# List-scheduled expert work, and seven block products instead of eight for the second expert matrix in two of three passes

## Chip, cores and metric

The kernel runs on one core of one Trainium2 chip. The metric is device time of one execution in microseconds (us). TensorE (PE) multiplies, VectorE (DVE), ScalarE (ACT) and GpSimd (POOL) do elementwise work, SyncE (SP) issues the DMAs.

## What is computed

```python
scores = scale * np.matmul(q, k.transpose(0, 1, 3, 2))       # 4 x 8 heads, 576 tokens, 64 wide
attn = np.matmul(scores * Dmat, v)                           # decaying causal retention
x = attn as (2304 tokens, 512)
h = x @ w_in                                                 # 512 -> 1024
solu = h * softmax(h); ln = layernorm(solu) * g_ln
x = ln @ w_out                                               # 1024 -> 512
for e in range(4):                                           # experts, all on every token
    h = np.maximum(x @ w1[e], 0.0)                           # first product, 512 -> 1024
    out += p[:, e:e + 1] * (h @ w2[e])                       # second product, 1024 -> 512
```

All is float32. Every operand of a large product is split in a high and a low part, and `mm3` adds three products for one (high by high, high by low, low by high).

## The kernel before

The 2304 tokens are 18 groups of 128 (`NG`), worked off in three passes of six groups. Passes are numbered 1 to 3 here (`p` is 0 to 2 in the code). A pass has a stage `h_mm` (x by `w_in`, softmax and norm, transposes by `t_mm`), a stage `x2_mm` (by `w_out`), and `experts`, which takes most of the time. The retention of groups 0 to 10 stands ahead of pass 1, interleaved by hand in the string `ORDER`; groups 11 to 17 are done at the start of the pass that needs them (`own_groups`).

**First product of an expert.** The token dimension, the input dimension and the hidden dimension are each cut in two, and the eight block products are replaced by seven with sums of blocks (Strassen-Winograd, `PRODUCTS`). On the weight side the sums are S1 to S4, on the token side T1 to T4. It goes in four quarters (`m` of `NM`), each of seven products of 2 x 3 matmuls of 384 columns: 168 matmuls. `l1` evicts them: ACT copies, DVE additions, then `relu_hi` on ACT and `relu_lo` on DVE make the split of h.

**Second product.** `l2_mm` multiplies a block of 128 tokens by all of `w2`: eight slices of the hidden dimension, three matmuls each, 512 columns. Six blocks make 144 matmuls. `l2_out` multiplies by the probability and adds to `acc`.

**Weights.** In every pass, and so three times, `w1_load` and `w1_ops` fetch `w1` (512 KB for each quarter), POOL forms S1 to S4, and ACT and DVE split the seven blocks into one of three slots of `wA`. `w2_ops` fetches 256 KB slices and splits them on ACT and POOL into `wB`. These operations are queued by hand between the products: `W1_SLOTS` and `W2_SLOTS` say after which product how many are issued. Every engine then works in the order of the code.

## Time and profile before

| | us |
|---|---|
| timed runs, median of 3 | 1056.38 |
| timed runs, lowest and highest | 1053.75, 1474.92 |
| profiled execution, first to last instruction (span) | 1052.0 |
| of it PE busy | 1029.9 (98%) |
| DVE, ACT, POOL busy | 537.4, 459.3, 346.7 |

The profile is of one execution. Its span leaves out what lies ahead of the first and behind the last instruction. Matmuls are pipelined, so their busy time overlaps: the cost of one is read from the distance of two starts, not from its duration.

### The profile page before, as it was taken

How to read it: one execution, taken by the hardware profiler on the slowest of the kernel's cores; microseconds unless marked ns; L12 is line 12 of the kernel's file. 1: busy time of each engine (PE TensorE's matmuls, PEld its weight loads, DVE VectorE, ACT ScalarE, POOL GpSimd, SP SyncE). 2: the span in 40 equal slices, each digit the busy share in tenths (PEclk: the TensorE clock that was granted, in tenths of full speed). 3: DMA queues.
4: the chain of work that ended last, by engine and by line, in shares of the span. 5: the costliest groups of instructions: out<-in, count | busy, mean ns of one | idle time of the engine just before them, and what ended most of it. 6: DMA issues, size and time to landing. Idle time of an engine off the chain costs nothing.

```text
span 1052.0 us, 15117 instructions
## 1 busy us (share of the span) xinstructions
PE 1029.9 (98%) x5996; PEld 929.6 (88%) x5996; DVE 537.4 (51%) x855; ACT 459.3 (44%) x872; POOL 346.7 (33%) x385
## 2 busy tenths in 40 slices
PE   5899999999999999999999999999999999999998
PEld 4788998998989888999898989988899989898996
DVE  6999764453635315565363544514556536354441
ACT  4478563342625206654262533403565426153430
POOL 2433443432433101443352334112143335233410
PEclk9999999999999999999999999999999999999999
DMA  9856531321212661112121212535412122121311
GB/s 348 340 208 221 198 123 60 90 64 67 81 40 81 254 266 72 41 54 67 61 80 41 80 60 90 200 141 208 203 41 61 60 71 70 40 89 56 88 39 50
DMA packets 35062, 118.56 MB, mean 113 GB/s; under 512 B 4144, under 2 KB 4144, under 8 KB 28848
## 3 DMA queue, kind: packets, MB, share of 16 engines
q1 hardware_dynamic: 34992, 117.60, 32.1%
q8 instruction: 47, 0.77, 0.3%
q14 instruction: 23, 0.19, 0.1%
HBM read 101.86 MB, written 15.73 MB: 112 GB/s over the span
## 4 chain that ended last, share of the span: by engine, by line
PE 92%; DVE 5%; DMA 2%; ACT 1%; issue 1%; SPq 0%; DVEq 0%; ACTq 0%
PE o L139 12%; PE o L140 12%; PE o L138 12%; PE l1x L138 6%; PE l1x L140 6%; PE l1x L139 6%; PE l1y L140 3%; PE l1y L139 3%; PE l1y L138 3%; PE x2ps L138 3%; PE x2ps L139 3%; PE x2ps L140 3%; PE hps L138 3%; PE hps L139 2%; PE hps L140 2%; PE l1z L140 2%
## 5 line engine op out<-in xcount | busy, mean ns | idle before, releaser
L140 PE MATMUL o<-wB,h 128*128 128x512 f32 x576 | 224.8, 390 | 0.0
L139 PE MATMUL o<-wB,h 128*128 128x512 f32 x576 | 224.7, 390 | 0.0
L138 PE MATMUL o<-wB,h 128*128 128x512 f32 x576 | 224.5, 390 | 0.0
L581 POOL TENSOR_TENSOR tmp<-tmp 128x256 f32<-128x256 f32 x192 | 156.2, 828 | 176.8 <-DVE wA L143 157.8
L143 POOL TENSOR_TENSOR wB<-tmp,wB 128x512 fp32r<-128x512 f32 x96 | 123.7, 1295 | 238.1 <-ACT wB L146 238.1
L146 ACT ACTIVATE wA<-tmp 128x512 fp32r<-128x512 f32 (+1 forms) x145 | 100.1, 704 | 173.3 <-DMA tmp<-in_w 110.6
L682 DVE SCALAR_TENSOR_TENSOR acc<-o,pr,acc 128x512 f32<-128x512 f32 x54 | 40.5, 751 | 204.5 <-PE o L140 204.5
L140 PEld LDWEIGHTS o<-wB,h 128*128 128x128 f32 x576 | 108.2, 188 | 22.4
L138 PEld LDWEIGHTS o<-wB,h 128*128 128x128 f32 x576 | 108.2, 188 | 22.0
L139 PEld LDWEIGHTS o<-wB,h 128*128 128x128 f32 x576 | 108.1, 188 | 21.7
L143 DVE TENSOR_TENSOR wA<-tmp,wA 128x512 fp32r<-128x512 f32 (+1 forms) x145 | 109.6, 778 | 4.5 <-ACT wA L146 4.5
L146 ACT ACTIVATE tmp<-l1x 128x384 f32<-128x384 f32 x96 | 47.1, 491 | 121.6 <-PE l1x L140 118.9
L138 PE MATMUL l1x<-xb,wA 128*128 128x384 f32 x288 | 96.7, 336 | 1.2 <-ACT tmp L146 1.2
L139 PE MATMUL l1x<-xb,wA 128*128 128x384 f32 x288 | 96.4, 335 | 0.0
L140 PE MATMUL l1x<-xb,wA 128*128 128x384 f32 x288 | 96.3, 335 | 0.0
L138 PE MATMUL x2ps<-h,wB 128*128 128x384 f32 x192 | 65.1, 339 | 0.4 <-DVE wA L377 0.4
L146 ACT ACTIVATE wB<-tmp 128x512 fp32r<-128x512 f32 x96 | 60.6, 631 | 9.9 <-DMA tmp<-in_w 9.9
L140 PE MATMUL x2ps<-h,wB 128*128 128x384 f32 x192 | 64.3, 335 | 0.0
L139 PE MATMUL x2ps<-h,wB 128*128 128x384 f32 x192 | 64.3, 335 | 0.0
L138 PE MATMUL l1y<-xa,wA 128*128 128x384 f32 x192 | 64.2, 335 | 0.0
L139 PE MATMUL l1y<-xa,wA 128*128 128x384 f32 x192 | 64.2, 335 | 0.0
L140 PE MATMUL l1y<-xa,wA 128*128 128x384 f32 x192 | 64.2, 334 | 0.0
(142 smaller groups left out, 1882.5 us busy)
## 6 DMA issues: line engine op xcount, KB each, us to landing
tmp<-in_w SPq DMA_DIRECT2D x48, 512.0 KB, 3.6
tmp<-in_w SPq DMA_DIRECT2D x96, 256.0 KB, 2.6
grps<-in_qkv SPq DMA_DIRECT2D x17, 1024.0 KB, 5.8
wA<-sin SPq DMA_DIRECT2D x8, 1024.0 KB, 6.9
wB<-sout SPq DMA_DIRECT2D x8, 1024.0 KB, 8.2
out<-acc SPq DMA_DIRECT2D x18, 256.0 KB, 2.1
grps<-in_qdec SPq DMA_DIRECT2D x16, 256.0 KB, 5.8
sin<-wA SPq DMA_DIRECT2D x4, 1024.0 KB, 7.7
```

Source lines behind the costliest of these rows:

```text
L138: nc.tensor.matmul(ps, lh, rh, start=first, stop=False, skip_group_check=more)
L139: nc.tensor.matmul(ps, lh, rl, start=False, stop=False, skip_group_check=more)
L140: nc.tensor.matmul(ps, ll, rh, start=False, stop=last, skip_group_check=more)
L143: (eng or nc.vector).tensor_tensor(out=dst, in0=src, in1=hi.bitcast(F32), op=ALU.subtract)
L146: nc.scalar.activation(out=dst, in_=src, func=AF.Copy)
L581: return lambda: nc.gpsimd.tensor_tensor(out=dst, in0=a, in1=b, op=op)
L682: nc.vector.scalar_tensor_tensor(out=a, in0=ps, scalar=sc, in1=a, op0=ALU.mult, op1=ALU.add)
```

## The change

**Order.** `nc` becomes a `Recorder`. From the second half of pass 1's `x2_mm` stage on, every operation is recorded with what it reads and writes; `flush` gives each a due time, counted back from when PE would need it, and issues them engine by engine, earliest due first, by a table of costs (`FIXED`, `RATE`). PE's own operations stay in the order of the code. The hand-made slots are gone.

**Pass 1** still computes the second product by eight block products. It forms and splits each `w1` quarter once, and stores the split blocks in DRAM (`w1_store`, 1792 KB for each quarter in runs of 1 KB). For `w2`, DVE adds S1 to S4 (`w2_next`, stored unsplit in runs of 512 bytes), and `w2_blocks` copies the three plain blocks from DRAM to DRAM.

**Passes 2 and 3** run `experts_s`. The first product is the same, from stored splits: one DMA of 256 KB for each of 28 products, 14 slots. The second product works on transposed tokens with seven block products for each of two output halves: 2 x 7 x 4 slices x 3 = 168 matmuls of 384 columns. Its weight blocks come unsplit from DRAM (14 of 256 KB, 6 slots) and are split again by ACT and POOL. Its token side needs T1 to T4 of h: eviction of the first product (`evict1`) grows by the subtractions into `Tf` and by splits of all seven blocks. `gather` multiplies by a row of probabilities and adds.

**Retention.** Groups 12 to 17 move from pass 3's start into pass 2's `h_mm` stage, and are stored in DRAM for pass 3.

```diff
+class Recorder:
...
+    def start(self):
+        self.ops = []
...
+    def flush(self, done=True):
+        ops, self.ops = self.ops, None if done else []
...
+        for op in ops:
+            op.after, op.due, op.at = [], None, clock
+            if op.engine == "PE":
+                op.due = clock
+                clock += op.cost
...
+        for op in reversed(ops):
+            due = min((s.due for s in op.after), default=None)
+            if due is None and op.engine != "PE":
+                due = op.at + SLACK
+            if due is not None:
+                due -= op.cost + LATENCY
+                op.due = due if op.due is None else min(op.due, due)
...
+        while len(order) < len(ops):
+            late = now + 1e-9
+            while waiting and waiting[0][0] <= late:
+                op = heapq.heappop(waiting)[2]
+                queue[op.engine].append((op.due, op.index, op))
...
+            for e in FIXED:
+                if free[e] > late or not queue[e] or (e == "SP" and self.dma > late + DEPTH):
+                    continue
+                can = [r for r in queue[e] if not (r[2].port and self.port > late)]
+                can = [r for r in can if all(busy.get(b, 0) <= late for b in r[2].banks)]
+                if e == "PE":
...
+                best = min(can)
+                queue[e].remove(best)
+                op = best[2]
+                moved = True
...
+                order.append(op)
...
+        for op in order:
+            op.call()
...
+SLACK = 12.0
+DEPTH = 2.0
...
+    ctx.enter_context(stack)
...
+    def open_pool(name, bufs):
+        stack.close()
+        new = stack.enter_context(tc.tile_pool(name=name, bufs=1, space=bass.MemoryType.PSUM))
+        width = 2048 // bufs
+        pool["a"] = [new.tile([P, width], F32, tag=f"a{i}", name=f"{name}_{i}") for i in range(bufs)]
+        pool["n"] = 0
...
+    def w1_store(s):
+        o = 3584 * (s % 3)
+        dst = s_w1[s].rearrange("p (b h t) -> h p b t", b=7, h=2)
+        for h in range(2):
+            src = wA[:, o + 1792 * h : o + 1792 * h + 1792].bitcast(F32)
+            nc.sync.dma_start(out=dst[h], in_=src.rearrange("p (b t) -> p b t", b=7))
+
+    def w2_blocks(e):
+        for m in range(2):
+            dst = s_w2[e][:, 3584 * m : 3584 * m + 1536].rearrange("p (a t) -> p a t", a=3)
+            nc.sync.dma_start(out=dst, in_=w2b[e, m].rearrange("a p t -> p a t"))
...
+    def w2_next(e, k):
+        raw = (w2s, area["wC"][:, 0:1024].rearrange("p (i t) -> p i t", i=2))[k % 2]
+        buf = area["wC"][:, 1024:2048]
+        s1, s2, s3, s4 = (buf[:, 256 * i : 256 * i + 256] for i in range(4))
+        a11, a21, a12, a22 = (raw[:, j, 256 * i : 256 * i + 256] for j in range(2) for i in range(2))
...
+        nc.sync.dma_start(out=raw, in_=w2[e, k::4].rearrange("a p t -> p a t"))
+        for j in range(2):
+            f = k + 4 * j
+            copy(wB[:, f, 0], raw[:, j])
+            low(wB[:, f, 1], raw[:, j], wB[:, f, 0], nc.gpsimd)
+        add(s1, a21, a22, ALU.add)
+        add(s3, a11, a21, ALU.subtract)
+        add(s2, s1, a11, ALU.subtract)
+        add(s4, a12, s2, ALU.subtract)
+        src = buf.rearrange("p (s m t) -> p s m t", s=4, m=2)
+        dst = s_w2[e].rearrange("p (m b k t) -> k p b m t", m=2, b=7, k=4)[k]
+        for m in range(2):
+            nc.sync.dma_start(out=dst[:, 3:7, m], in_=src[:, :, m])
...
     def experts(p):
         for e in range(E):
-            s0 = p * E * NM + e * NM
-            if e > 0:
...
+            s0 = e * NM
+            for k in range(4):
+                w2_next(e, k)
...
-            bg = w1b + w2b
+                        w1_next(s + 2)
...
+            w1_next(last + 3)
+            w2_blocks(e)
...
+    def w1_slot(n):
+        o = 512 * (n % 14)
+        return wA[:, o : o + 512]
+
+    def w2_slot(n):
+        c = (n + 3) % 6
+        w = wA[:, 7168 + 1024 * c :] if c < 4 else area["wC"][:, 1024 * (c - 4) :]
+        return w[:, 0:1024].rearrange("p (s t) -> p s t", s=2)
...
+    def w1_fill(n):
+        e, (m, i) = n // 28, L1_SEQ[n % 28]
+        a = PRODUCTS[i][0]
+        nc.sync.dma_start(out=w1_slot(n).bitcast(F32), in_=s_w1[e * NM + m][:, 512 * a : 512 * a + 512])
...
+    def w2_load_s(n):
+        e = n // 14
+        m, i = (L2_LAST if e == E - 1 else L2_SEQ)[n % 14]
+        o = 512 * (7 * m + PRODUCTS[i][0])
+        nc.sync.dma_start(out=w2_slot(n)[:, 1].bitcast(F32), in_=s_w2[e][:, o : o + 512])
+
+    def w2_split(n):
+        dst = w2_slot(n)
+        raw = dst[:, 1].bitcast(F32)
+        copy(dst[:, 0], raw)
+        low(dst[:, 1], raw, dst[:, 0], nc.gpsimd)
...
+        for n in range(14):
+            w1_fill(n)
+        for n in range(6):
+            w2_load_s(n)
+            w2_split(n)
...
+        xs = [t[:, 0:BLK] for t in pool["a"]]
+        ys = [t[:, 0:BLK] for t in bt]
+        zs = [sbank[:, 0:BLK]]
+        banks = {1: xs, 5: ys, 2: zs, 6: xs, 4: xs, 3: ys, 7: xs}
...
+        def mms(kind, k, i, ks):
+            if (k, i) not in at:
+                at[k, i] = used[kind]
+                used[kind] += 1
+            n = at[k, i]
+            w = w2_slot(n) if kind == "w2" else w1_slot(n).rearrange("p (s t) -> p s t", s=2)
+            b = PRODUCTS[i][1]
+            more = i in (6, 4, 3, 7)
+            nk = 2 if kind == "w1" else 4
+            r = xpart if kind == "w1" else hop
+            for kk in ks:
+                sl = slice(P * kk, P * kk + P)
+                mm3(
+                    bank(k, i), (w[:, 0, sl], w[:, 1, sl]), (r(b, kk, 0), r(b, kk, 1)), not more and kk == 0,
+                    kk == nk - 1, more,
+                )
+            return n if ks[-1] == nk - 1 else None
...
+        def bsplit(m, i, ps):
+            relu(bgrp(m, 0)[:, i], ps)
+            stt(bgrp(m, 1)[:, i], ps, bgrp(m, 0)[:, i].bitcast(F32))
+
+        def tsplit(m, i):
+            copy(tgrp(m, 0)[:, i], Tf[:, i])
+            low(tgrp(m, 1)[:, i], Tf[:, i], tgrp(m, 0)[:, i], nc.gpsimd)
+
+        def gather(e, m, blk, ps):
+            j = blk % 2
+            dst = acct[:, m, blk]
+            half = pb[:, j * BLK : j * BLK + BLK]
+            if e == 0:
+                nc.vector.tensor_tensor(out=dst, in0=ps, in1=half, op=ALU.mult)
+                return
+            q = qf[:, blk % 2]
+            nc.vector.tensor_tensor(out=q, in0=ps, in1=half, op=ALU.mult)
+            nc.vector.tensor_tensor(out=dst, in0=dst, in1=q, op=ALU.add)
...
+        def evict1(k, m, i):
+            x, y, z = bank(k, 1), bank(k, 5), bank(k, 2)
+            if i == 1:
+                copy(t1r, x)
+            elif i == 5:
+                copy(t5r, y)
+            elif i == 2:
+                add(z, z, t1r)
+                relu(bf[:, 0], z)
+                bsplit(m, 0, z)
+            elif i == 6:
+                copy(t2r, x)
+            elif i == 4:
+                stt(Tf[:, 3], x, Tf[:, 2])
+                bsplit(m, 2, x)
+                tsplit(m, 3)
+            elif i == 3:
+                add(y, y, t2r)
+                relu(bf[:, 1], y)
+                stt(Tf[:, 0], y, bf[:, 0])
+                tsplit(m, 0)
+            elif i == 7:
+                add(y, x, t5r)
+                stt(Tf[:, 1], y, bf[:, 1])
+                stt(Tf[:, 2], y, Tf[:, 0])
+                bsplit(m, 1, y)
+                tsplit(m, 1)
+                tsplit(m, 2)
+
+        def evict2(k, e, m, i, final):
+            x, y, z = bank(k, 1), bank(k, 5), bank(k, 2)
+            if i == 1:
+                copy(t1r, x)
+            elif i == 5:
+                copy(t5r, y)
+            elif i == 2:
+                add(z, z, t1r)
+                gather(e, m, 0, z)
+            elif i == 6:
+                copy(t2r, x)
+            elif i == 4:
+                gather(e, m, 2, x)
+                if m == 1 and e + 1 < E:
+                    pb_load(p, e + 1)
+            elif i == 3:
+                add(y, y, t2r)
+                gather(e, m, 1, y)
+            elif i == 7:
+                c = bf[:, 0] if final else y
+                add(c, x, t5r)
+                gather(e, m, 3, c)
+
...
+            for m in range(2):
+                tail = e == E - 1 and m == 1
+                a, b, c = range(3), range(3, 4), range(4)
+                if m == 0:
+                    seq = [(1, a), (4, c), (5, a), (2, a), (1, b), (5, b), (2, b), (6, c), (3, c), (7, c)]
+                elif tail:
+                    seq = [(i, c) for i in (1, 5, 2, 6, 4, 7, 3)]
+                else:
+                    seq = [(i, c) for i in (1, 5, 2, 6, 4, 3, 7)]
+                for i, ks in seq:
+                    if i == 4:
+                        todo.append(prev)
+                    else:
+                        todo.append(("w2", k, e, m, i, ks))
+                prev = ("w2", k, e, m, 4, c)
+                if tail:
+                    todo.append(prev)
...
+            for kind, kk, ee, m, i, ks in todo:
+                n = mms(kind, kk, i, ks)
...
+                if kind == "w1":
+                    evict1(kk, m, i)
+                    if n + 14 < 28 * E:
+                        w1_fill(n + 14)
+                else:
+                    evict2(kk, ee, m, i, ee == E - 1 and m == 1)
+                    if n + 6 < 14 * E:
+                        w2_load_s(n + 6)
+                        w2_split(n + 6)
...
         feed[f"in_{name}"] = a
         args.append(nc.dram_tensor(f"in_{name}", a.shape, mybir.dt.from_np(a.dtype), kind="ExternalInput").ap())
-    args.append(nc.dram_tensor("out_0", (NT, DM), F32, kind="ExternalOutput").ap())
```

TensorE in passes 2 and 3, where an expert's first product ends and its second begins. `o`, `l1x`, `psX`, `b` and `sbank` are PSUM accumulators; `h`, `hx` and part of `wB` hold the token side afterwards. Before:

```order
L138 MATMUL o<-wB,h_3507 128x512
L139 MATMUL o<-wB,h_3507 128x512
L140 MATMUL o<-wB,h_3507 128x512
L138 MATMUL l1x<-xb,wA 128x384
L139 MATMUL l1x<-xb,wA 128x384
L140 MATMUL l1x<-xb,wA 128x384
```

After:

```order
L144 MATMUL psX_0_4004<-wB,wA 128x384 x9
L144 MATMUL psX_3_4007<-xb,wA 128x384 x6
L144 MATMUL b_67<-h_554,wC 128x384 x6
L144 MATMUL b_67<-h_983,wC 128x384 x3
L144 MATMUL sbank<-wB,wC 128x384 x9
L144 MATMUL psX_0_4004<-wB,wA 128x384
L144 MATMUL psX_0_4004<-hx,wA 128x384
L144 MATMUL psX_0_4004<-wB,wA 128x384
L144 MATMUL b_67<-h_983,wC 128x384 x3
```

Matmuls of 512 columns with six token blocks became matmuls of 384 columns, and the last product of the first matrix (by `xb`) stands behind nine matmuls of the second.

SyncE in pass 1, from the first expert on. Before:

```order
L599 DMA tmp<-in_w 128x512 x2
L260 DMA sout_97<-wB 128x2048
L571 DMA tmp<-in_w 128x1024
L260 DMA sout_99<-wB 128x2048
L599 DMA tmp<-in_w 128x512 x6
L571 DMA tmp<-in_w 128x1024 x4
```

After, at the second expert (`sw_3` to `sw_5` are split `w1` quarters, `sw_0_137` and `sw_1_138` the sums and blocks of `w2`):

```order
L144 DMA sw_3_124<-wA 896x1x256 x2
L144 DMA tmp<-in_w 128x1024
L144 DMA sw_0_137<-wCf 128x4x128 x2
L144 DMA sw_4_125<-wA 896x1x256 x2
L144 DMA sw_1_138<-in_w2b 128x3x512
L144 DMA sw_0_137<-wCf 128x4x128
L144 DMA tmp<-in_w 128x1024
L144 DMA sw_0_137<-wCf 128x4x128
L144 DMA tmp<-in_w 128x2x512
L144 DMA sw_1_138<-in_w2b 128x3x512
L144 DMA sw_5_126<-wA 896x1x256 x2
```

Stores of splits and sums, and copies inside DRAM, now stand between the loads of the weights.

ScalarE in a quarter of the first product of passes 2 and 3. Before:

```order
L146 ACTIVATE tmp<-l1y 128x384
L146 ACTIVATE tmp<-l1x 128x384
L621 ACTIVATE h_560<-l1z 128x384
L146 ACTIVATE wB<-tmp 128x512
L621 ACTIVATE h_6201<-l1y 128x384
L146 ACTIVATE wB<-tmp 128x512
L146 ACTIVATE tmp<-l1x 128x384
L621 ACTIVATE h_6201<-tmp 128x384
L146 ACTIVATE tmp<-l1y 128x384
```

After:

```order
L144 ACTIVATE tmp<-psX_0_4004 128x384
L144 ACTIVATE tmp<-b_68 128x384
L144 ACTIVATE h_554<-tmp 128x384 x2
L144 ACTIVATE wB<-b_67 128x384
L144 ACTIVATE wB<-sbank 128x384
L144 ACTIVATE tmp<-psX_0_4004 128x384
L144 ACTIVATE wB<-psX_3_4007 128x384
L144 ACTIVATE tmp<-sbank 128x384
L144 ACTIVATE h_554<-tmp 128x384
L144 ACTIVATE tmp<-b_68 128x384
L144 ACTIVATE h_983<-tmp 128x384
L144 ACTIVATE tmp<-psX_1_4005 128x384
```

The splits of weights (`wB<-tmp`) left this place, and the copies and relus that make all seven token blocks (`h`, `wB`, `tmp`) took their places.

## Rows read from the trace of the kernel before

**Rows 1.** The page's part 1: busy time, share of span, instructions.

```profile
span 1052.0 us, 15117 instructions
PE 1029.9 (98%) x5996; PEld 929.6 (88%) x5996; DVE 537.4 (51%) x855; ACT 459.3 (44%) x872; POOL 346.7 (33%) x385
```

**Rows 2.** Windows: length, busy us of each engine, granted clock, DMA share, GB/s.

```profile
20.00:120.00 100.00, 94.86 (x897) 82.44 (x893) 90.74 (x129) 69.84 (x133) 33.73 (x36) 1.00 0.65 243
140.00:390.00 250.00, 250.00 (x1256) 226.20 (x1255) 108.69 (x175) 92.49 (x180) 84.08 (x86) 1.00 0.30 103
462.00:702.00 240.00, 240.00 (x1225) 217.66 (x1223) 107.91 (x176) 93.76 (x183) 86.46 (x88) 1.00 0.28 93
803.00:1052.00 249.00, 244.63 (x1231) 221.56 (x1230) 108.61 (x177) 93.42 (x182) 82.35 (x84) 1.00 0.20 64
```

**Rows 3.** Chain that ended last, shares of the span by engine.

```profile
PE 92%; DVE 5%; DMA 2%; ACT 1%; issue 1%; SPq 0%; DVEq 0%; ACTq 0%
```

**Rows 4.** Timeline of PE, and of all engines at the end: start, duration.

```profile
138.87 0.44 PE L138 MATMUL l1x<-xb,wA 128*128 128x384 f32 x1 [1.16 <-ACT tmp L146]
...
599.74 0.34 PE L138 MATMUL l1x<-xb,wA 128*128 128x384 f32 x1
...
611.01 0.34 PE L140 MATMUL l1x<-xb,wA 128*128 128x384 f32 x1
...
1044.29 0.39 PE L139 MATMUL o<-wB,h 128*128 128x512 f32 x1
...
1047.24 0.39 PE L140 MATMUL o<-wB,h 128*128 128x512 f32 x1
1047.67 0.75 DVE L682 SCALAR_TENSOR_TENSOR acc<-o,pr,acc 128x512 f32<-128x512 f32 x1 [4.69 <-PE o L140]
1048.44 0.33 SPq L684 DMA_DIRECT2D out<-acc  x1
```

**Rows 5.** Groups by form: count, busy us, mean ns of one, idle before.

```profile
L143 POOL TENSOR_TENSOR wB<-tmp,wB 128x512 fp32r<-128x512 f32 x96 | 123.7, 1295 | 238.1 <-ACT wB L146 238.1
...
L146 ACT ACTIVATE wB<-tmp 128x512 fp32r<-128x512 f32 x96 | 60.6, 631 | 9.9 <-DMA tmp<-in_w 9.9
...
L624 DVE SCALAR_TENSOR_TENSOR h<-tmp,h 128x384 fp32r<-128x384 f32 x48 | 38.1, 795 | 28.9 <-ACT h L621 26.3
...
L631 DVE TENSOR_TENSOR l1z<-l1z,tmp 128x384 f32<-128x384 f32 x48 | 27.0, 563 | 20.9 <-ACT tmp L146 16.7 <-PE l1z L140 4.1
...
L621 ACT ACTIVATE h<-l1x 128x384 fp32r<-128x384 f32 x48 | 23.6, 492 | 18.3 <-PE l1x L140 15.8
...
L146 ACT ACTIVATE xb<-acc 128x384 fp32r<-128x384 f32 x18 | 8.7, 518 | 1.3 <-DVE acc L519 1.3
...
L519 POOL TENSOR_TENSOR acc<-tmp,acc 128x384 f32<-128x384 f32 x6 | 6.1, 1017 | 28.6 <-DVE acc L519 28.6
```

**Rows 6.** DMA: GB/s in 40 slices, packets of the queue, issues with median us to landing.

```profile
GB/s 348 340 208 221 198 123 60 90 64 67 81 40 81 254 266 72 41 54 67 61 80 41 80 60 90 200 141 208 203 41 61 60 71 70 40 89 56 88 39 50
...
q1 hardware_dynamic: 34992, 117.60, 32.1%
...
tmp<-in_w SPq DMA_DIRECT2D x48, 512.0 KB, 3.6
tmp<-in_w SPq DMA_DIRECT2D x96, 256.0 KB, 2.6
grps<-in_qkv SPq DMA_DIRECT2D x17, 1024.0 KB, 5.8
```

**Rows 7.** Who waited for whom: us in total, times, longest.

```profile
DVE h L624 <- ACT h L621: 108.6, 101, 1.7
```

**Rows 8.** Chain in order of time, pass 3's retention: start, us, what.

```profile
715.33 1.02 PE o L355 x16
...
724.06 1.02 PE o L355 x16
```

More of the change, by code (lines that the diff above doesn't have):

```diff
@@ L60, with spans @@
 """
+LATENCY = 0.12
+ISSUE = 0.06
+FIXED = {"PE": 0.0135, "ACT": 0.13, "DVE": 0.16, "POOL": 0.36, "SP": 2.0}
+RATE = {"PE": 1 / 2400, "ACT": 0.93e-3, "DVE": 1.03e-3, "POOL": 1.82e-3, "SP": 4 * P / 300e3}
+ENGINE = {"tensor": "PE", "scalar": "ACT", "vector": "DVE", "gpsimd": "POOL", "sync": "SP"}
+def spans(ap):
+    dims = [tuple(d) for d in ap.ap]
+    start = ap.offset
+    if ap.space == bass.MemoryType.DRAM and (dims[0][1] != P or dims[0][0] == 0):
+        return ap.name, [(0, 1 << 40)]
+    width = dims[0][0]
+    start %= width
+    runs, size = [start], 1
+    inner = sorted((d for d in dims[1:] if d[1] > 1 and d[0] > 0), key=lambda d: d[0])
+    for step, n in inner:
+        if step == size:
+            size *= n
+        else:
+            runs = [r + step * i for r in runs for i in range(n)]
+    return ap.name, [(r, r + size) for r in runs]
@@ L63, in retention_solu_moe, with __init__, __getattr__ @@
+class Issuer:
+    def __init__(self, rec, name, engine):
+        self.rec, self.name, self.engine = rec, name, engine
+    def __getattr__(self, kind):
+        if self.rec.ops is None:
+            return getattr(getattr(self.rec.nc, self.name), kind)
+        return lambda *args, **kw: self.rec.record(self.name, self.engine, kind, args, kw)
+SLACK = 12.0
+DEPTH = 2.0
+TRACE = []
 @with_exitstack
@@ L305, in att_qk @@
         qt, kt = (t[:, i : i + 512].rearrange("p (n t) -> p n t", n=NP) for i in (0, 512))
-        qk = [psB.tile([P, NP, P], F32, tag="b", name=f"qk{a}") for a in range(2)]
+        qk = [quad(next_b()) for a in range(2)]
         for n in range(NP):
@@ L636, in l1 @@
         if i == 1:
[L637 to L638 removed]
+            x = next_a()[:, 0:BLK]
+            y, z = (next_b()[:, 0:BLK] for _ in range(2))
             steps[s] = (x, y, z)
```

437 lines of the change are left out of this document (324 added, 113 removed).

## Prediction

> **What bounds the kernel now.** I read the page's busy times first. PE is busy 98% of the span, and no other engine more than 51% [rows 1]. Busy time alone doesn't make a bound, so I read the chain of waits next: 92% of it is PE, 5% DVE [rows 3]. Then the windows by stage. From 140 us on PE is busy for the whole of a window (250.00 of 250.00, 240.00 of 240.00), while DVE, ACT and POOL stand near 44, 38 and 35% [rows 2]. The last window misses 4.4 us, which is the end: a last matmul at 1047.24, one DVE operation of 0.75 us and the output's DMA [rows 4]. Unhidden waits lie ahead of 140 us, among them 1.16 us at 138.87 [rows 2, 4]. The granted clock is 1.00 in every one of these windows, which is the 2.4 GHz level. So in the part that the change rewrites, time is the number of matmuls times their distance. There is no idle PE time that a better order could win back, beyond that 1.16 us; the scheduler alone is worth about nothing here. What can pay is fewer PE columns, and what can cost is any engine or DMA that no longer keeps up.
>
> **Price of a matmul.** The starts at 599.74 and 611.01 are 65 matmuls of 384 columns apart, 11.27 / 65 = 0.1734 us each. Those at 1044.29 and 1047.24 are 13 of 512 columns apart, 2.95 / 13 = 0.2269 us [rows 4]. The saving is not the full eighth, since a narrower matmul carries more fixed time per column (0.452 ns against 0.443).
>
> **Removed and added on PE.** Second product of one expert and pass: before 6 x 8 x 3 = 144 x 0.2269 = 32.67 us, after 2 x 7 x 4 x 3 = 168 x 0.1734 = 29.13 us. That is 3.54 us, eight times (four experts, two passes): 28.3 us off. The operand shapes (128x128 weights, 384 columns) are those of the first product, so I take its distance as it is. An expert of these passes goes from 168 x 0.1734 + 32.67 = 61.8 to 58.3 us. Pass 1 keeps its matmuls. The retention that moves from pass 3 to pass 2 is the same PE work: 0. Its operands have the same distance from load to use as they had in pass 3, where one group came every 9 us (715.33, 724.06) against a load of 5.8 us [rows 6, 8]; a stall of 0 to 6 us is possible, since two DMAs of `wB` now stand ahead of the third group's load on SP. I take 0.
>
> **ACT, DVE and POOL in passes 2 and 3.** For one quarter of a first product (42 matmuls, 7.28 us of PE), ACT now does 8 evictions from PSUM at 0.492 and 4 splits from SBUF at 0.518: 6.0 us, 83% [rows 5]. DVE does 10 operations at 0.563: 5.6 us, 77%. POOL does 4 subtractions at 1.017: 4.1 us. Over a whole expert (58.3 us), with the second product's evictions (6 copies, about 22 DVE operations) and the 14 splits of `w2` blocks (0.631 on ACT, 1.295 on POOL), ACT has 24.0 + 3.0 + 8.8 = 35.8 us, DVE 22.5 + 12.8 = 35, POOL 16.3 + 18.1 = 34. All fit, near 60%. What goes away there, three times splitting `w1`, is off the path.
>
> **The handover between the two products** is the new wait on the path, eight times. T1 of the last slice comes from the last quarter's product 7 by a DVE addition (0.563), a DVE subtraction (0.563), an ACT copy (0.518) and a POOL subtraction (1.017, or 1.295 as the wider one has): 2.7 to 2.9 us and four handoffs. PE has 9 + 6 + 9 + 9 + 3 = 36 matmuls in between, 6.2 us. So 3.3 us are left for the operations queued ahead on three engines. One operation ahead in each queue (0.56, 0.63, 1.3) fits; two don't. Bounds: 0, and about 2 us each. I take 0.3, or 2.4 us in all, near the lower end, because the trace's present handoffs of this kind cost PE nothing after 140 us [rows 2]. Behind a late T1 stands PE itself, in its fixed order, and no work of another expert can pass.
>
> **DMA in passes 2 and 3.** 42 blocks of 256 KB and 384 KB of probabilities for each expert are 11.4 MB in 58.3 us: 196 GB/s. The slices show up to 348 GB/s [rows 6]. A block lands 2.6 us after its issue; a `w1` slot is refilled 14 products (14.6 us) ahead, a `w2` slot 6 products (12.5 us), from which the split takes another 1.9. Cost 0 while SP issues on time; if that cover goes, see the third rival.
>
> **DMA in pass 1.** An expert there loads 4.2 MB, stores 7.3 MB of splits and 2.1 MB of sums, and copies 1.6 MB: 15.2 MB beside 61.8 us, 246 GB/s, where the trace moved 93 to 103. The windows give 103 / 0.30 = 343 and 243 / 0.65 = 374 GB/s at a full share [rows 2], so by bytes 41 to 44 us of 61.8. But those packets have 117.6 MB / 34992 = 3.4 KB in the mean [rows 6]; the stores have 1 KB and 512 bytes, which no row shows. By bytes the cost is 0. If every packet took as long as the mean one now (0.321 x 16 x 1052 / 34992 = 0.154 us), some 13,600 of them would need 131 us, 69 us too long in each expert. I stay near the bytes, since windows with different mixes agree within a tenth, and take 1 us for the first expert, where the stores of `w_out` fall too.
>
> **End.** The last eviction is now two DVE operations (0.563, then 0.6 to 0.8 with both inputs in SBUF) instead of 0.75: +0.5 us.
>
> **The sum.** 1052.0 - 28.3 + 2.4 + 1.0 + 0.5 = 1027.6 us of span. The median of the runs lies 4.4 us above the span, the lowest 1.8; with 4.4 the time is 1032.0.
>
> **Rivals.** First, handoffs slow the first product. ACT and DVE now alternate: addition, two relus, subtraction, copy, and then POOL. In each quarter ACT may idle 7.28 - 6.0 = 1.27 us before PE waits. Now a DVE eviction waited for its relu 1.1 us on average (108.6 us, 101 times) [rows 7], which costs nothing at today's load and is about the whole margin at the new one. If 0.25 to 0.75 us is lost in each of 32 quarters, 8 to 24 us come back: 1040 to 1056. Against it: the new order issues by due time, and the window's engines are idle half the time now [rows 2]. A DVE operation with both inputs in SBUF took 795 ns, against 563 for one with an input in PSUM [rows 5]. The Trainium skill ("SBUF — State Buffer", "Who interferes with whom") calls this an exclusive lock between GpSimd and such operations, held for a whole instruction. By that rule the eight added ones of an expert could each wait 1.295 us, 10 us more on DVE; that alone would still fit into 58.3, and the trace's +0.23 us agrees with a weaker form.
>
> Second, pass 1 becomes bound by its stores, and the result is **slower than before**. If the 9.4 MB of small runs move at half the windows' 343 GB/s, an expert needs 9.4 / 0.172 + 5.8 / 0.343 = 72 us against 61.8, 10 us more; four experts make 40 us, and the time 1072. It decides when the mean rate falls below 246 GB/s; SP then blocks on a store, and behind it stand the loads of the next quarter. For it speaks that neither run length is in the trace; against it that 28% of the rate is to spare.
>
> Third, small loads don't overlap. If each block waited for the one before, 43 x 2.6 = 112 us would stand against 58.3, 428 us over eight experts, about 1460. The 348 GB/s of the first slice speak against it, since one 256 KB load in 2.6 us is 101 GB/s. The Trainium skill ("DMA: Bandwidth & Descriptors", "Measured") advises batching DMAs to 1 MiB or more for 75% of peak, which speaks against this change's 256 KB; the trace's overlapped loads don't follow it.
>
> **How the numbers follow.** Two per cent, 21 us, is about what a measurement of this kernel can tell from no change; the line is 1035.2. The forecast (1024 to 1035, small stalls) gets 0.56, handoffs (1036 to 1056) 0.24, stores (above 1056, mostly 1060 to 1110) 0.14, serial loads 0.02, better than 1024 (the 1.16 us back, no stall, and runs near the lowest) 0.04. Faster by over 2% takes the forecast nearly whole and the last: 0.58. Same: 0.26. Slower: 0.16. The range 1024 to 1056 holds the first two cases, 0.80.
>
> **What would show it.** PE's distance stays 0.173 us in the second product of passes 2 and 3, with an expert near 58.3 us. PE's idle time after 140 us stays under 7 us, and where it is not, the waits name it: POOL or ACT at the first T1 or T2 product (handover), ACT or DVE within quarters (first rival), DMA on `wA` or `wB` in pass 1 with a DMA share near 1 (second). DMA shares of about 0.7 in pass 1 and 0.55 in passes 2 and 3 would confirm the loads. The prediction is wrong if an expert of pass 1 is longer than 63 us, or one of the later passes longer than 60.

## The result and the profile after

The changed kernel takes 1038.97 us (median of four runs, 1038.56 to 1042.08) where the kernel before takes 1056.18 on the same chip. The ratio is 0.985, with a 95% interval of 0.9828 to 0.9872. One run of the kernel before took 1474.92 us and is not in the ratio. The forecast was 1032.0, so 17.2 of the 24 us arrived. The profiled execution is the longest of the four (1042.08), and the one before was the shortest of its runs (1053.75), so their spans differ by 11.7 us only. The same kernel once more (control, `a2_same`) took 1039.16 us, ratio 0.9852 (0.9834 to 0.9871), and was profiled at 1037.51.

The page of the changed kernel, against [rows 1] and the queue line of [rows 6]: PE is still busy 97% of the span, every other engine has more work, and the DMA moves nearly twice the bytes.

```profile
span 1040.3 us, 17080 instructions
PE 1008.3 (97%) x6188; PEld 947.0 (91%) x6188; DVE 617.3 (59%) x1038; ACT 526.9 (51%) x1032; POOL 445.6 (43%) x433
q1 hardware_dynamic: 122704, 225.70, 65.2%
```

To see where the time went I cut both traces at the start of each expert's second product. Windows of the kernel before, one expert and the two stretches that hold a change of pass (columns as in [rows 2]):

```profile
225.83:287.69 61.86, 61.86 (x314) 56.18 (x314) 28.73 (x46) 25.05 (x48) 22.99 (x25) 1.00 0.22 69
349.55:487.46 137.91, 137.80 (x762) 124.51 (x761) 64.78 (x111) 61.36 (x113) 33.72 (x47) 1.00 0.36 136
673.04:828.13 155.09, 155.09 (x1065) 139.54 (x1065) 74.97 (x127) 66.69 (x126) 44.19 (x56) 1.00 0.39 145
```

The same windows of the changed kernel, in order of time: three intervals of pass 1, the change to pass 2, an interval of pass 2, the change to pass 3.

```profile
165.13:229.31 64.18, 62.89 (x314) 55.95 (x313) 40.83 (x64) 26.59 (x50) 27.87 (x28) 1.00 0.95 305
229.31:292.86 63.55, 62.85 (x313) 55.97 (x313) 44.50 (x68) 27.10 (x53) 30.79 (x29) 1.00 0.85 271
292.86:357.19 64.33, 62.66 (x313) 56.09 (x313) 39.33 (x65) 23.92 (x46) 21.05 (x20) 1.00 0.76 248
357.19:521.76 164.57, 161.15 (x1129) 144.22 (x1129) 72.62 (x127) 67.49 (x132) 41.91 (x51) 0.99 0.58 209
580.27:638.77 58.50, 58.50 (x337) 58.21 (x337) 34.42 (x63) 32.95 (x69) 34.85 (x31) 1.00 0.64 196
697.28:830.11 132.83, 130.90 (x722) 123.44 (x722) 70.79 (x125) 69.20 (x131) 42.22 (x51) 1.00 0.54 187
```

Every interval was 61.86 us before. In passes 2 and 3 it is 58.5, with PE busy throughout: the gain is there. Pass 1 has the same work on PE and takes 2 us more for each expert. The change to pass 2 now holds the retention that stood in the change to pass 3, so only their sum compares: 297.4 against 293.0. In us, forecast and measured:

| stretch | forecast | first profile | control |
|---|---|---|---|
| up to the first second product | 0 | +1.2 | -1.9 |
| three intervals of pass 1 | +1.0 | +6.5 | +6.6 |
| six intervals of passes 2 and 3 | -19.4 | -20.1 | -20.1 |
| the two changes of pass | -3.2 | +4.4 | +2.8 |
| from the last second product on | -2.7 | -3.6 | -3.6 |
| span | -24.4 | -11.7 | -16.3 |

(The forecast of six intervals is 6 x (0.3 - 3.54); the changes of pass hold one more such expert, and the end another with 0.5 more.) The whole shortfall lies in pass 1 and in the changes of pass, 13 us in the first profile and 12 in the control.

Who waits there: PE's waits in the changed kernel (us, times, longest), without those of its first 140 us.

```profile
PE sbank L144 <- POOL tmp L144: 2.4, 1, 2.4
...
PE b L144 <- POOL wB L144: 1.3, 2, 0.7
PE b L144 <- DVE h L144: 1.2, 2, 0.7
...
PE psA L144 <- DVE h L144: 1.1, 1, 1.1
PE b L144 <- ACT xb L144: 1.1, 1, 1.1
```

No line names a DMA. `psA` holds the two `x` banks of the first product, accumulators in PSUM that PE fills in turn. The wait on psA is at 342.50 us in pass 1. The timeline of DVE just before it (start, duration):

```profile
336.18 1.67 DVE L144 SCALAR_TENSOR_TENSOR h<-tmp,h 128x384 fp32r<-128x384 f32 x1 [0.34 <-ACT h L144]
337.78 1.54 DVE L144 TENSOR_TENSOR wCf<-wCf 128x256 f32<-128x256 f32 x4
339.24 0.56 DVE L144 TENSOR_TENSOR b<-b,tmp 128x384 f32<-128x384 f32 x1
...
341.90 0.55 DVE L144 SCALAR_TENSOR_TENSOR h<-psA,h 128x384 fp32r<-128x384 f32 x1
```

The four sums `wCf`, whose results nobody needs before pass 2, and a split of `w1` (at 340.83) stand ahead of the evictions; the last of these, `h<-psA`, frees PE's bank only at 342.4. So there were three candidates for pass 1: the bytes of the stores (DMA share 0.76 to 0.95), the place that the scheduler gives to work without a hurry, and the number of banks that can absorb a late eviction.

### The profile page after: what moved, and what is told of

The parts are those of the page before. It is cut to its first block, busy times and chain, and to the rows that moved or that the text cites. A ratio compares the mean times of both kernels' runs of the same rounds, so it can differ in the third digit from the quotient of the medians.

```text
span 1040.3 us, 17080 instructions
## 1 busy us (share of the span) xinstructions
PE 1008.3 (97%) x6188; PEld 947.0 (91%) x6188; DVE 617.3 (59%) x1038; ACT 526.9 (51%) x1032; POOL 445.6 (43%) x433
## 4 chain that ended last, share of the span: by engine, by line
PE 51%; issue 1%; DVE 0%; ACT 0%; POOL 0%; POOLq 0%; ACTq 0%
PE psX L144 26%; PE b L144 16%; PE sbank L144 6%; PE psA L144 3%; DVE acc L144 0%; POOL acc L144 0%; DVE stats L144 0%; ACT psA L144 0%; ACT acc L144 0%; DVE tmp L144 0%; ACT xb L144 0%; ACT xa L144 0%; ACT tmp L144 0%; POOLq L144 0%; ACTq L144 0%
## 5 line engine op out<-in xcount | busy, mean ns | idle before, releaser
L144 POOL TENSOR_TENSOR h<-tmp,h 128x384 fp32r<-128x384 f32 x128 | 128.7, 1015 | 95.9 <-ACT h L144 82.1
L144 PE MATMUL b<-xa,wA 128*128 128x384 f32 x672 | 132.8, 335 | 2.3 <-DVE h L144 1.2
L144 PE MATMUL b<-wB,h 128*128 128x512 f32 x576 | 133.0, 390 | 1.3 <-POOL wB L144 1.3
L144 PEld LDWEIGHTS b<-wB,h 128*128 128x128 f32 x576 | 107.8, 188 | 24.2 <-POOL wB L144 2.2
L144 POOL TENSOR_TENSOR wA<-wA 128x512 fp32r<-128x512 f32 x74 | 97.2, 1321 | 68.0 <-ACT wA L144 65.0
L144 PEld LDWEIGHTS b<-xa,wA 128*128 128x128 f32 x672 | 117.7, 188 | 3.5 <-DVE h L144 2.1
L144 PE MATMUL psX<-xb,wA 128*128 128x384 f32 x576 | 112.6, 336 | 0.1
L144 PEld LDWEIGHTS psX<-xb,wA 128*128 128x128 f32 x576 | 100.4, 188 | 2.7 <-DVE b L144 2.3
L144 PE MATMUL b<-h,wB 128*128 128x384 f32 x480 | 85.1, 336 | 0.0
L144 PEld LDWEIGHTS b<-h,wB 128*128 128x128 f32 x480 | 83.0, 188 | 0.1
```

The lines of the kernel that those rows point to most:

```text
L144: op = Op(engine, lambda: call(*args, **kw), FIXED[engine] + rate * n, port)
```

## The experiments

The kernels ran in three groups, each on one chip: the held loads, the stores of the first expert, eight products and the recorded order; the control, slack, banks and both; and last the three edits with the banks opened earlier, the stores of the last expert, eight products with four banks, and the handover's order. Across groups the ratios to the kernel before are compared. The control first.

> The changed kernel once more, unaltered, as the control of the three others on their chip, and to see which waits of its first profile come back. Every theory: 1038 to 1039.5 us; the wait at 399 to 401 ahead of `sbank` (2.4 us) and the 1.3 us wait near 340 come back, the stretch at half clock behind the first of them may not.

Measured: 1039.16 us, as above. The waits for `sbank` (1.4 us) and psA (1.1) came back, the half clock behind the first did not.

**Are the stores to blame?** Two kernels keep the order of every other instruction and issue the stores of one expert only (the second has `s < 3 * NM`; the stores of `w2` and the blocks likewise). Passes 2 and 3 then read that expert's splits for all four, so the weights of the other three are left out.

```diff
 nc.sync.dma_start(out=dst[h], in_=src.rearrange("p (b t) -> p b t", b=7))
+if s >= NM:
+    nc.ops[-1].call = lambda: None
```

> Edit: the order of all instructions stays, but the stores of splits, sums and blocks are issued for the first expert alone (42 of 56 store DMAs left out); passes 2 and 3 read the first expert's splits for every expert, so the weights of the other experts are missing from the result. Theory (pass 1 pays for the DMA traffic of the stores: share 0.93 from 140 to 262 us): the second and third interval from one second product to the next, 63.55 and 64.33 us, fall to 61.9 to 62.4, the DMA share there below 0.5, POOL's waits for `wB` and PE's behind them go, time 1034.5 to 1035.5. Rival (the order of DVE, ACT and POOL, with the four sums of w2 on DVE, is what delays PE): the intervals stay at 63.3 or above and the time at 1038 or above.

> Edit: the order of all instructions stays, but splits, sums and blocks are stored for the last expert alone; passes 2 and 3 read its splits for every expert, so the weights of the others are missing from the result. In the first interval (64.2 us, with PE's two waits of 0.8 us for `wB` at 168 us), the stores of the first experts share the DMA with those of the decoded w_out. Store theory: both waits go, the first interval falls to 62.6 or below, time 1036 to 1037. Order theory (POOL splits w2 late because ACT and POOL do w1's work first, and sums wait for one buffer): the waits shrink by less than half, the first interval stays at 63.4 or above, time 1038 or above. The third interval, whose stores are there again, stays at 64.2 by either.

Measured: 1037.58 (ratio 0.9838, 0.982 to 0.9856) and 1039.49 us (0.985, 0.983 to 0.987). Windows of the first kernel, second and third interval, and then of the second kernel, first interval:

```profile
227.88:290.68 62.80, 62.74 (x314) 56.02 (x314) 42.14 (x68) 27.12 (x53) 29.15 (x29) 1.00 0.26 84
290.68:354.96 64.28, 62.65 (x314) 56.07 (x314) 40.04 (x65) 23.59 (x46) 20.07 (x20) 1.00 0.24 81
```

```profile
166.32:230.53 64.21, 62.91 (x314) 55.98 (x314) 40.73 (x64) 26.61 (x50) 26.77 (x28) 1.00 0.27 81
```

With the DMA share down from 0.95 to 0.27 the first interval stays at 64.21, and the third at 64.28. Only the second fell, by 0.8 to 0.9 us (62.80 here and 62.78 in the second kernel), where the store theory said 62.4 at most and its rival 63.3 at least. So the store theory falls for the first and third interval, and 0.8 us of the second is what the stores cost. What takes the rest these two kernels don't show; the order is left as a candidate.

**What is the scheduler's own share?** The next kernel keeps the scheduler and the moved retention, and goes back to eight products without sums of `w2` and without stores.

```diff
-        w1_store(s)
...
-            experts_s(p)
+            experts(p)
...
```

> Edit: the list scheduler orders all work from the first expert on and the retention stays in pass 2, as in the changed kernel, but the experts of all passes take eight block products in the second product as before the change, split w1 and w2 anew, and nothing is stored (the result is complete, in one output). The prediction's claim that the scheduler alone is worth about nothing gives 1054 to 1059, with 61.8 to 62.3 us an expert in every pass, so that the seven products with all they bring are worth the whole 17 us net. Rival A (the scheduler itself gains by filling waits): 1050 or below. Rival B (the scheduler's order costs pass 1 its 2 us an expert even without stores): 63.5 us an expert and 1070 or above.

Measured: 1068.28 us, ratio 1.0132 (1.0113 to 1.0152), slower than before the change. All intervals within a pass are 62.4 to 62.8 us. My claim (about nothing) and rival A fall; rival B has the sign, with 0.5 to 1.0 us an expert in place of 1.6. One of its waits, in the first interval shown below (start, duration): DVE takes up a split of `w1` just before the eviction `h<-psA` comes ready, and PE's next weights for psA wait for that.

```profile
272.06 0.96 DVE L144 TENSOR_TENSOR wA<-tmp,wA 128x768 fp32r<-128x768 f32 x1 [1.04 <-ACT wA L144]
272.93 0.55 DVE L144 SCALAR_TENSOR_TENSOR h<-psA,h 128x384 fp32r<-128x384 f32 x1
...
273.54 1.00 PEld L144 LDWEIGHTS psA<-xa,wA 128*128 128x128 f32 x6 [0.46 <-DVE h L144]
```

The same kernel was then run with four narrow `x` banks for the experts.

```diff
+            nc.flush()
+            open_pool(f"psY{p}", 4)
+            nc.start()
             experts(p)
...
```

> Edit: the kernel with eight products in every pass under the list scheduler (1068 us, 62.4 to 62.8 us an expert) with four narrow `x` banks for the experts in place of two wide ones; the stages' batches are cut before the experts of passes 2 and 3, so only later experts of a pass compare. Theory (the greedy order lets a split of 0.8 to 1.5 us start just before an eviction comes ready; two banks turn that into a wait of PE, four take it up): the second to fourth expert of each pass fall to 61.9 to 62.2 us. Rival (the loss has nothing to do with the `x` banks): they stay at 62.4 to 62.8.

Measured: 1057.34 us, ratio 1.0023 (1.0012 to 1.0034). Windows with two banks (one interval of pass 1, the change to pass 2, one interval of pass 2), and with four:

```profile
225.83:288.41 62.58, 62.44 (x313) 56.05 (x313) 28.26 (x47) 25.29 (x49) 24.37 (x26) 1.00 0.21 68
350.81:517.39 166.58, 161.83 (x1129) 144.41 (x1129) 84.31 (x134) 72.34 (x134) 52.80 (x64) 0.99 0.48 173
580.23:642.98 62.75, 62.61 (x314) 56.05 (x313) 28.69 (x47) 25.34 (x49) 23.64 (x25) 1.00 0.22 68
```

```profile
224.67:286.56 61.89, 61.89 (x314) 56.20 (x314) 28.61 (x47) 25.19 (x49) 23.24 (x24) 1.00 0.23 69
348.42:511.71 163.29, 159.99 (x1130) 142.92 (x1129) 80.88 (x132) 71.08 (x133) 50.06 (x61) 1.00 0.48 175
573.57:635.43 61.86, 61.86 (x314) 56.17 (x313) 28.50 (x47) 25.19 (x49) 23.24 (x24) 1.00 0.22 68
```

With four banks every expert is back at 61.86 us (61.89 once), the figure of the hand-made order, which has two. So the greedy order delays evictions, and two banks turn each delay into a wait of PE. Passes 2 and 3 of the changed kernel have four, and don't show it. The change to pass 3, which lost the retention, shrank here from 155.09 to 134.26 us, by 20.8; the change to pass 2, which received it, grew from 137.91 to 163.29, by 25.4. So the retention costs 4.6 us more in its new place than in its old one, with eight products as well, and PE's idle time there is 3.3 of them. No run has the scheduler with the retention in its old place; but in the change to pass 3, which the scheduler ordered too, PE is idle for 0.3 us only.

**Due times, banks, and both.** Three kernels sent with the control:

```diff
-SLACK = 12.0
+SLACK = 60.0
```

> Edit: the due time of work that nothing waits for (the sums of w2 and their stores, and the stores of w1) is put 60 us behind its place in the program in place of 12; the work stays. Theory of due times (in pass 1 the four sums stand ahead of evictions on DVE, as at 337.78 us, and PE waits 1.1 us for the bank): the sums move into the second products, the wait of 1.3 us near 340 and the ones near 286 and 334 go, the second and third interval fall from 63.55 and 64.33 to 62.3 to 62.9, time 2 to 3 us under the control. Rival (the splits of w1, 0.8 to 1.5 us long, are what stands ahead of evictions; sums only seem to): intervals and time within 0.7 us of the control. DMA theory: the stores move too, but their bytes stay, so no change either.

Measured: 1036.53 us, 2.6 under the control, ratio 0.9832 (0.981 to 0.9854; the intervals of the two overlap). The second and third interval:

```profile
227.08:289.14 62.06, 62.06 (x313) 56.16 (x313) 39.35 (x68) 26.28 (x50) 25.55 (x26) 1.00 0.83 273
289.14:352.24 63.10, 62.76 (x313) 56.12 (x313) 37.97 (x66) 24.09 (x46) 21.58 (x20) 1.00 0.75 242
```

They fell by 1.6 and 1.2 us against the control's 63.67 and 64.25, at nearly the same DMA share (0.86 and 0.76 in the control); the last is 0.2 above what I expected. On DVE three of the four sums now come behind `h<-psA`.

```diff
     def experts(p):
+        nc.flush()
+        open_pool("psY", 4)
+        nc.start()
...
```

> Edit: in pass 1 the first products take their `x` bank from four tiles of 512 in place of two of 1024, as passes 2 and 3 do; the two wide tiles come back before the retention. Nothing else. Theory (with two banks an eviction that is 1 us late stops PE, with four it doesn't; passes 2 and 3 lose only 0.2 us an expert): the waits of PE on psA go (1.3 us near 340, 0.3 us elsewhere), intervals 64.18 / 63.55 / 64.33 fall to 63.9 / 62.8 / 62.7, time 2 to 2.5 us under the control. Rival (the delayed engine, not the bank, sets the pace, and PE meets the next wait on `b` or `h` instead): within 0.7 us of the control.

> Edit: the three together: the loads of `wB` held behind those of the retention groups, 60 us of slack, four `x` banks in pass 1. If the three causes are separate, their gains add up: 1.2 + 2.5 + 1 (banks and slack share the wait near 340) gives 4 to 5.5 us under the control, 1033.5 to 1035, faster than both kernels. If pass 1 is bound otherwise (the bytes of the stores, or the splits), 1 to 2 us.

Measured: 1050.13 (0.9952, 0.9934 to 0.997) and 1047.82 us (0.9936, 0.9919 to 0.9953), 11 and 9 us over the control. The banks did what they should: second and third interval 62.27 and 63.24, with slack 62.25 and 62.53. But the first grew to 74.2 and 75.2, with PE waiting 5.4 us for ACT's splits into `wB`. The edit had a part that I had overlooked: the flush cuts the scheduler's batch, so the loads and splits of the first expert's `w2` can no longer be drawn forward beside the stage before it. The next kernel opens the four banks earlier, where a batch begins anyway.

```diff
             xb_region()
+            open_pool("psY", 4)
             nc.start()
             w1_ops(0)
...
```

> Edit: loads of `wB` held behind the retention's, slack of 60 us, and the four narrow `x` banks of pass 1 opened before the work of the second half of the first stage is recorded, so that the first expert's batch isn't cut as in the run before. If the causes are separate: first interval 63.5 to 64 (no 10 us wait for the splits of w2), then 62.0 to 62.5 each, transition 161.2; time 1033 to 1035, against 1039.2 of the control and 1036.5 with slack alone. Rival (a cut batch was not the cause of the 10 us; four banks let PE run ahead of w2's splits): the first interval stays above 70 and the time above 1044.

Measured: 1034.76 us, ratio 0.9811 (0.979 to 0.9831); the interval doesn't meet the control's. Its three intervals of pass 1:

```profile
165.20:229.07 63.87, 62.45 (x313) 56.02 (x313) 42.90 (x71) 27.93 (x53) 32.89 (x32) 1.00 0.97 313
229.07:291.38 62.31, 62.29 (x314) 56.14 (x313) 40.46 (x69) 25.84 (x49) 23.34 (x26) 1.00 0.88 278
291.38:353.64 62.26, 62.26 (x314) 56.12 (x313) 36.48 (x64) 23.76 (x46) 20.35 (x20) 1.00 0.74 237
```

With the pool opened where a batch begins the 10 us are gone, so they came with the cut. This kernel beats both, by 4 us the changed one (0.0041 of 1055); it also holds the loads of `wB`, and its change to pass 2 takes 161.30 us. What is left of pass 1 is the first interval, with two waits of 0.7 us for POOL's splits into `wB`: neither the stores, nor the banks, nor the slack moved them. The trace leads one step further (start, duration):

```profile
162.84 1.55 DVE L144 TENSOR_TENSOR wCf<-wCf 128x256 f32<-128x256 f32 x4
164.41 0.37 SPq L144 DMA_DIRECT2D wCf<-in_w  x1
169.45 3.67 POOL L144 TENSOR_TENSOR wB<-wCf,wB 128x512 fp32r<-128x512 f32 x2
171.50 0.98 PE L144 MATMUL b<-wB,h 128*128 128x512 f32 x3 [0.72 <-POOL wB L144]
```

The load of a `w2` slice is issued as soon as DVE has done the sums of an earlier slice (`wCf`), and POOL's split of it comes late. In the two kernels without sums and stores the last such load is issued at 157.5 to 157.9 us, and neither wait is there; in the one without stores of this expert, but with sums, both are. That points at the sums; no run takes away the sums alone, so the cause stays open.

**Does the queue of `wB` make the third group late?**

```diff
         att_load(g)
+        if nc.ops:
+            loads[g] = nc.ops[-2:]
...
                     nc.sync.dma_start(out=dst, in_=s_out[i - 1].rearrange("p (f s t) -> p f s t", f=2, s=2))
+                    if own:
+                        nc.ops[-1].before |= set(loads[OWN[i + 1]])
```

> Edit: each load of `wB` in pass 2 is held behind the load of one retention group (the first behind the third group's, the next behind the fourth's, and so on), so that none stands ahead of it on SP; nothing else changes. Queue theory: the third group's load, issued at 394.3 and landed at 402.7 us beside four 1 MB loads of wB, then has the DMA to itself and lands near 399; PE's 2.42 us wait ahead of `sbank` goes, and with it the 3.4 us at half clock that follow (1.7 us lost). Time 1039.0 -> 1034.5 to 1035.5. Rival (the load is late because `tmp` comes free late, and its own 1 MB is what is waited for): the wait stays above 1.2 us and the time stays at 1037.5 or above. A third outcome, above 1039: the loads of wB or of a later group become the late ones.

Measured: 1037.55 us, ratio 0.9838 (0.9821 to 0.9856). The first profile has the load issued at 394.32 and POOL starting on it at 402.70, 8.4 us later, with the wait of PE behind it:

```profile
394.32 0.37 SPq L144 DMA_DIRECT2D tmp<-in_qkv  x1
```

```profile
402.70 1.04 POOL L144 TENSOR_TENSOR tmp<-tmp,tabs 128x512 f32<-128x512 f32 x1 [23.83 <-DMA tmp<-in_qkv]
...
403.80 0.68 PE L144 MATMUL sbank<-tmp 128*64 128x64 f32 x16 [2.42 <-POOL tmp L144]
```

The control has 391.31 and 398.68 (7.4 us, a wait of 1.4); this kernel 393.11 and 400.00:

```profile
401.10 0.69 PE L144 MATMUL sbank<-tmp 128*64 128x64 f32 x16 [0.93 <-POOL tmp L144]
```

So the load takes 6.9 us with nothing of `wB` ahead of it, and PE still waits 0.93 us. The change of pass fell from the control's 162.92 to 161.50, 1.4 us. The queue was a part; the larger part is that the load is issued only 7 us before PE wants the data (401.10 - 0.93 - 393.11; the same 7 us in the first profile and in the control). In the first profile the last matmul that reads this buffer ends 0.2 us ahead of the load's issue:

```profile
392.99 1.09 PE L144 MATMUL b<-tmp 128*64 128x128 f32 x16
```

The rival was nearer.

**Does the order matter in passes 2 and 3?** The stage's instructions are issued as they were recorded.

```diff
-        for op in order:
+        for op in sorted(order, key=lambda op: op.index) if plain else order:
             op.call()
```

> Edit: the expert stages of passes 2 and 3 are issued in the order in which they are recorded (each eviction behind its product, each split behind its load) in place of the scheduler's order; instructions and data are the same, pass 1 and the retention keep the scheduler's order. Theory (the order matters here, since ACT and POOL must not stand before a load that was issued just ahead): ACT waits about 2 us for DMA at each of 14 splits of w2 blocks an expert, with evictions queued behind; each second product of 29.1 us grows by 5 to 14 us, time 1080 to 1150. Rival (engines near 57% busy leave room for any order): experts stay below 59 us and the time within 3 us of 1039.

Measured: 1158.15 us, ratio 1.0981 (1.0957 to 1.1006), 8 us over my upper end. ACT's waits in pass 2, and PE's, of this kernel:

```profile
ACT wA L144 <- DMA wA<-sw: 42.8, 22, 7.5
...
ACT wC L144 <- DMA wC<-sw: 17.6, 8, 7.3
```

```profile
PE psX L144 <- ACT tmp L144: 30.4, 12, 6.1
```

Experts take 73 to 76 us, with ACT, DVE and POOL no busier than in the changed kernel: an in-order engine that waits for a load holds every eviction behind it. That wait is some 10 us an expert (30.4 in three), and at a granted clock of 0.93 to 0.95 PE is busy for 61 to 65 us in place of 58.5. Against this recorded order the scheduler is worth 15 to 17 us an expert. That can't be set beside the result for eight products, which were measured against an order made by hand; no such order of seven was run.

**Where is the handover's cost?**

```diff
-seq = [(1, a), (4, c), (5, a), (2, a), (1, b), (5, b), (2, b), (6, c), (3, c), (7, c)]
+seq = [(i, c) for i in (1, 4, 5, 2, 6, 3, 7)]
```

> Edit: in the second product of passes 2 and 3 the first slice takes its products whole, in the order 1, 4, 5, 2, 6, 3, 7, in place of the order that splits 1, 5 and 2 so that the last quarter's operands are read late. PE then has 27 matmuls (4.7 us) between the last quarter's product 7 and the first use of its T1, in place of 36 (6.2 us). Theory (the chain of 2.7 to 2.9 us plus up to one queued operation on each engine, 5 to 5.5 us in all, is what the order hides): 0.5 to 1.2 us more at each of 8 handovers, experts 59.0 to 59.7 us, time 1043 to 1048. Rival (the chain is over before either point): experts stay at 58.5, the time within 1 us of the control.

Measured: 1039.86 us, ratio 0.9853 (0.9827 to 0.9879): the time shows nothing. In the profiled execution (1040.96) the first second product started 5.3 us later than the control's (167.29 against 162.02), with the same instructions up to there, which is more than the edit can give (8 x 0.26 = 2.1 us). The intervals tell more:

```profile
580.56:638.80 58.24, 58.24 (x337) 58.24 (x337) 33.41 (x63) 33.12 (x69) 35.37 (x31) 1.00 0.67 197
```

58.24 is 336 x 0.1733: no wait is left at all. My theory falls. The 0.26 us that the changed kernel loses at each handover comes from the split order itself: with 9 matmuls in place of 12 ahead of product 4, PE reaches the last quarter's bank before DVE has read product 7 out of it. The trace of the changed kernel names it (us, times, longest, three experts), and this kernel has no such line:

```profile
PEld psX L144 <- DVE b L144: 0.9, 3, 0.3
```

## Why the prediction was right, and where it was off

**What held, and what of it is luck.** The time lies in the range 1024 to 1056, but in the part that belongs to the first rival (1036 to 1056, chance 0.24), not in the forecast's own (1024 to 1035, 0.56); "faster by over two per cent" had 0.58, and 1.5 came. That part of the range was made for losses in passes 2 and 3, which lost no more than forecast; the losses came in pass 1 and at the changes of pass. By its own signs the prediction was wrong in pass 1, where an expert was not to be longer than 63 us (64.18, 63.55 and 64.33 came), and PE was idle for 9.5 us from 140 us to its last matmul, not under 7.

**Right: the price and the place of the gain.** 28.3 us off in eight second products, less 2.4 for handovers, made 3.24 us an expert; 3.35 were measured. The three helpers had been given 35.8, 35 and 34 us of an expert, and took 33, 34 and 35; the loads 196 GB/s, and moved 196. That an engine at 60% hides its work held there.

**The handover (0.3 each) had the right size by luck, and the wrong cause:** not a late T1, but the bank of product 4 (0.26).

**Wrong: "the scheduler alone is worth about nothing".** I had read from [rows 2] that there was no idle time to win, and took this as if nothing could be lost either. With eight products it costs 14 us (ratio 1.0132), the moved retention included: by the profile 6.5 in the nine intervals within passes, 8.0 in the two changes of pass (166.58 and 134.40), and a little less at both ends. With four banks the intervals lose nothing, the changes of pass lose the 4.6 of the moved retention, and 2.4 us are left in all (1.0023). It sorts by due time and doesn't wait for what is about to come ready, so a split or sum that has just become possible goes ahead of an eviction that is nearly so.

**Wrong: pass 1 as "DMA in pass 1", 1 us, and nothing else.** Measured 6.5. Of that, 0.8 us went with the stores, in the second expert and not in the first, so the term's size is luck. The second rival, stores, had the right place and the wrong mechanism: the DMA share was 0.95 in place of the 0.7 expected, but the first and the third interval lost the same at 0.27 and 0.24. The step that failed is that the prediction gave pass 1 no cost on DVE, ACT and POOL. What happened is close to the first rival's mechanism, an eviction that comes late because other work stands ahead of it, in a place where I hadn't put it: I charged it to passes 2 and 3, which have four banks, and not to pass 1, which kept two while DVE's work grew from 28.7 to 40.8 us in an interval. With slack and banks 3.7 of the control's 6.6 us went (64.24 + 63.67 + 64.25 against 63.87 + 62.31 + 62.26), 3.1 of them with slack alone; 2.0 of what remains are in the first interval, cause open.

**Under-sized: the retention that moves, "I take 0" of 0 to 6.** The bound held, the choice didn't. The wait came at the very load that I had named, 2.42 us in the first profile and 1.41 in the control. In all, the changes of pass lost 7.6 (4.4 + 3.2) and 6.0 us against the forecast. Most of it is the retention in its new place: the change to pass 2 took 164.57 us, and 162.92 in the control, where 137.91 + 20.8 = 158.7 were due, so 5.9 and 4.2. Near 2 us are in the change to pass 3 (132.83 against 134.26 - 3.54 = 130.7), where PE is idle for 1.93 us; 1.1 of it is the wait on ACT's `xb` in the list of waits above, at 802 us. No run was made on that part.

**The third rival, small loads,** did not come: loads of 256 KB moved those 196 GB/s, and no wait of PE names a DMA. The 348 GB/s that the prediction held against it are of loads of 0.5 to 1 MB for the most part, so they said little on 256 KB.

**From span to time.** The 4.4 us that the sum adds are not a constant: each run's time lies 1.8 us above its own span, and 2.6 was the distance of the profiled run from the median.

**The rule on ports.** The prediction weighed the Trainium skill ("SBUF — State Buffer", "Who interferes with whom"): a DVE operation with two inputs in SBUF contends with a GpSimd instruction that reads SBUF, and the lock is exclusive. Passes 2 and 3, groups by form (count, busy, mean ns):

```profile
L144 DVE TENSOR_TENSOR acc<-acc,tmp 128x384 f32<-128x384 f32 x24 | 17.0, 709 | 0.8
L144 DVE TENSOR_TENSOR b<-b,tmp 128x384 f32<-128x384 f32 x25 | 14.1, 565 | 16.6 <-PE b L144 13.6 <-ACT wC L144 3.0
```

The trace agrees: 709 against 565 ns in the mean. One by one, 18 of the 24 took 0.55 to 0.56 us, some of them beside work on POOL, and six took 0.94 to 1.47; those of the second line took 0.55 to 0.57 throughout. So a few are held for long, and not each for a little. By the mean it is 1.2 us for eight of them, not the 10 of the rule at its worst, and it hides.

## What to carry to other kernels

An engine without idle time says that an order can win nothing; it doesn't say that a new order can lose nothing. Before trusting a greedy list scheduler, count the banks between PE and the evictions, give work without a consumer a due time that is truly late, and see where its batches are cut. Later due times and four banks, with some loads held back, were worth 4 us here; a cut in the wrong place cost 10. With eight products, two banks and the moved retention the scheduler cost 14 us, with four banks 2.4. And a DMA share near 1 is no wait: look at who waits, and let a kernel without the traffic decide.

## What the runs showed of the hardware

A short wait of PE was followed by half its clock, though not each time. In the first profile the 2.42 us wait at 401 was followed by a granted clock of 0.50, the 1.2 GHz level (windows; the clock is the third column from the end):

```profile
400.00:404.00 4.00, 1.58 (x32) 1.34 (x30) 0.69 (x1) 0.60 (x1) 1.30 (x2) 1.00 1.02 420
...
405.00:406.00 1.00, 1.00 (x14) 1.00 (x11) 0.00 (x0) 0.37 (x1) 0.00 (x0) 0.50 1.05 442
...
408.00:409.00 1.00, 1.00 (x5) 0.81 (x5) 0.33 (x1) 0.00 (x0) 0.00 (x0) 1.00 0.92 336
```

At the same place, behind a wait of 2.0 us with slack of 60, it was 0.50 too (400 to 402 us); behind one of 1.9 us, with the stores of the first expert alone, and of 1.41 us in the control, it stayed at 1.00. In the run with the cut batch and four banks, PE was busy 8.63 of 14 us at 174, and the clock was low throughout:

```profile
174.00:188.00 14.00, 8.63 (x20) 5.55 (x19) 7.33 (x10) 2.62 (x4) 6.82 (x7) 0.51 0.93 296
```

The time up to the first expert differs from execution to execution with the same instructions (first second product at 162.02 to 167.29 us), as much as most of these experiments are worth. The clock differs on the way (between 45 and 50 us 1.00 in the control and 0.66 in the first profile, between 15 and 25 us 0.83 and 1.00); how much of the difference it makes no run shows. That is why intervals were compared here, and not times alone.
